# Sparse attention and a feed-forward layer on one core: where and when the later weights are converted, and in which order the first loads go out

## The chip, the cores and the metric

The kernel runs on one core of a Trainium2 chip. A core has five engines with a queue of instructions each: TensorE (PE in the profile, with its weight loads as PEld), VectorE (DVE), ScalarE (ACT), GpSimd (POOL) and SyncE (SP, which only issues DMAs). Sixteen DMA engines move data between DRAM and the on-chip memory; SP, ACT and POOL each issue into a queue of their own. The metric is the device time of one execution in microseconds; of several executions the median counts.

## The reference, cut to what matters

```python
# q, k, v: (4 batches, 8 heads, 768 positions, 64); blocks of 32 positions, 24 to a batch
scores = scale * np.matmul(q, k.transpose(0, 1, 3, 2))
mask = np.abs(blk_i - blk_j) <= 1                       # a query block sees its neighbours,
mask = mask | (blk_i == 0) | (blk_j == 0) | (blk_i == 23) | (blk_j == 23)   # the two end blocks,
for qb in range(24):                                    # and three sampled blocks
    for kb in sampled_blocks[qb]:
        mask[qb*32:(qb+1)*32, kb*32:(kb+1)*32] = True
attn = softmax(np.where(mask, scores, -1e9))
x = (attn @ v) as 3072 tokens x 512
h = x @ w_in                                            # 512 x 2048
g = np.maximum(h, 0.0) + np.log1p(np.exp(-np.abs(h)))
return g @ w_out                                        # 2048 x 512
```

`w_in` and `w_out` are double precision; everything else is single. The first and the last query block of each batch see all keys.

## The kernel before, in words

**Attention.** A batch has six *places*: groups of four query blocks (the last has two), and the first and last query block are handled together as a seventh *set* of the batch, marked `whole`. That makes 28 sets. Each set is worked in two *units* of four heads, 56 in all, and each unit in three *pieces*: `score_piece` (`scores`: matmuls on the neighbours straight from the keys `kT` and on a gathered tile `kg`, then the masking reduction on DVE), `value_piece` (`exponents` on ACT, then `values`, matmuls with `vg`) and `transpose_piece` (`normalise`, `transposes`, whose copies from PSUM go half to ACT and half to DVE). Pieces of neighbouring units overlap: score of unit n + 2 beside values of unit n.

POOL gathers. For each query block it copies three sampled key blocks from `kT` into `kg` (L461); the end blocks' keys are copied for the first two places of each batch (L451). For V it issues an indirect DMA per query block (L498) into the `vg` tile of the set, with row numbers from `ix` (`make_index`). Beside that SP loads the neighbours' rows of V (L489) and, into partitions 96 to 127, block 0 (L492); the fourth group of 32 rows of each gather is the last block of V. `vg` has two buffers in the pool `wk`.

**Feed-forward.** Tokens are worked in eight tiles of 384 (three places each). A hidden *unit* is one tile times one of sixteen slices f of the 2048 hidden columns: 12 matmuls `h` (L208 to L210), the softplus on ACT and DVE, and 9 matmuls `o` (L265 to L267) three units later (`LEAD`). Each single-precision operand is split into a high and a low part, and three products are taken. The *first pass* runs slices 0 to 5 (`EARLY`) of all eight tiles: 48 units, between which the attention pieces that make the next tile of x are placed (`due`); partial outputs go to DRAM (`yD`), and so do the x tiles (`xD`). The *second pass* runs slices 6 to 15 on x tiles read back: 80 units. In program order the loop over j emits `first_half(j)`, attention pieces that are due, `second_half(j)`, more pieces.

**Weights.** A *half* is one slice of one matrix, 128 x 512 double-precision words, 512 KB. `Weights` turns it into two single-precision parts: a raw load (L125), two ACT operations (`words`, L132 and L135), three DVE operations (`assemble`, L140, L144, L147), an integer add on POOL (L151), a cast on ACT (`high`, L157) and a subtraction (`low`, L163: DVE for the early slices, POOL for the later ones). `step` alternates between load, high and words for successive halves, and low and assemble. The 12 early halves are converted from the start on, one step per call of `convert` (one after each attention piece, two per j), their loads issued on ACT's queue. When they are done, their buffers are given up and the second batch's keys are loaded in their place (`kT[1]`). The 20 later halves are converted after the attention, when its memory is free, at 3.4 steps per unit (`HALVES`), straight into tiles of the pool `w2`.

**The start.** 22 attention pieces go before the first hidden unit (`needs[0]`). The order of the first loads is written out by hand ahead of the loop.

Of the kernel before, what the change touches and what calls it, by code (L numbers as in the profile page):

```python
# [19 lines left out]
BLOCK = 32  # L20
# [15 lines left out]
HALVES = 3.4  # L36
# [3 lines left out]
def sparse_attention_ffn(  # L40
# [20 lines left out]

    nc = tc.nc
    B, NG, P, NP, NI, _ = q.shape
    NB = k.shape[1]
# [29 lines left out]
    convctx = ctx.enter_context(ExitStack())  # L94
# [6 lines left out]
    yD = [dram.tile([P, DM], F32, name=f"yD{n}") for n in range(len(order))]  # L101

# [4 lines left out]
    class Weights:  # L107
# [5 lines left out]
        def __init__(self, halves, engine, ahead, late):  # L113

            self.halves, self.engine, self.ahead, self.late = halves, engine, ahead, late
            self.at = 0
            self.raw, self.t, self.r = {}, {}, {}
# [4 lines left out]
        def load(self, h):  # L122
            f, which = self.halves[h]
            raw = pools["conv"].tile([P, DM], I64, tag="raw", name=f"raw{which}{f}", bufs=self.ahead + 1)
            self.engine.dma_start(out=raw, in_=w_out[f * P : (f + 1) * P, :] if which else w_in[f])  # L125
            self.raw[h] = raw

        def words(self, h):
            f, which = self.halves[h]
            self.t[h] = pools["conv"].tile([P, DM], F32, tag="wt", name=f"wt{which}{f}", bufs=self.late + 1)  # L130

            nc.scalar.activation(self.t[h], self.view(h, F32)[:, :, 1], AF.Abs)  # L132
# [4 lines left out]
        def assemble(self, h):  # L137
            ti = self.t[h].bitcast(I32)
# [4 lines left out]

            nc.vector.tensor_scalar(  # L144
                out=ti, in0=ti, scalar1=3, scalar2=0x3FFFFFFF, op0=ALU.logical_shift_left, op1=ALU.bitwise_and
            )
            nc.vector.scalar_tensor_tensor(  # L147
# [3 lines left out]
            nc.gpsimd.tensor_tensor(out=ti, in0=ti, in1=self.r[h], op=ALU.add)  # L151

        def high(self, h):
            f, which = self.halves[h]
            pool = w1 if f < EARLY else pools["w2"]
            W[which, f] = [pool.tile([P, DM], F32R, name=f"w{x}{which}{f}") for x in range(2)]
            nc.scalar.copy(out=W[which, f][0], in_=self.t[h])  # L157

        def low(self, h):
            f, which = self.halves[h]  # L160
            hi, lo = W[which, f]
            eng = nc.gpsimd if f >= EARLY else nc.vector
            eng.tensor_tensor(out=lo, in0=self.t[h], in1=hi.bitcast(F32), op=ALU.subtract)  # L163
# [12 lines left out]

        def done(self):
            return self.at >= 2 * (len(self.halves) + self.ahead + self.late)
# [121 lines left out]
    pools["conv"] = convctx.enter_context(tc.tile_pool(name="conv", bufs=2))  # L300
# [9 lines left out]
    ixf = ac.tile([P, NB], F32, name="ixf")  # L310
    ix = ac.tile([P, B, NB], I32, name="ix")
# [15 lines left out]
    nc.vector.memset(ixf[NR * BLOCK : P], float((LAST - NR) * BLOCK))  # L327
    nc.vector.tensor_copy(out=iuf, in_=iu)
    nc.vector.tensor_copy(out=iof, in_=io)
# [19 lines left out]
    def make_index():  # L349

        for s in range(NR + 1):
            rows = slice(s * BLOCK, (s + 1) * BLOCK)
            if s == NR:
                nc.vector.tensor_scalar(
# [532 lines left out]
```

## Time and profile before

| | |
|---|---|
| time, median of 3 runs | 914.66 us (912.77 to 917.05) |
| the profiled execution | 920.34 us, span 918.6 us |
| PE busy | 814.6 us (89%) |
| PE weight loads | 676.6 us (74%) |
| DVE busy | 601.7 us (66%) |
| ACT busy | 466.8 us (51%) |
| POOL busy | 248.7 us (27%) |
| DMA | 127.44 MB, mean 139 GB/s |
| mean granted TensorE clock | 0.949 |

Busy times are of one execution, and the shares are of its span. A share over the whole span averages stages with different limits: the start with attention alone, the first pass with attention and hidden units mixed, a stretch in which the later weights are converted, and the rest of the second pass. Where a view lists waits, it gives the waiting instruction, what ended the wait, the total, the count and the longest.

### The profile page before, as it was taken

To read this page: it belongs to the slowest core of one execution; us is meant where nothing else is said; L and a number is where in the kernel's file an instruction comes from. 1 tells how busy PE (TensorE), PEld (TensorE's weight loads), DVE (VectorE), ACT (ScalarE), POOL (GpSimd) and SP (SyncE) were. 2 spreads that over 40 slices of the span, in tenths; PEclk is the share of its full clock that TensorE was granted. 3 is DMA by queue.
4 is the path that set the end of the run, shared out by engine and by line. 5 is a ranking of instruction groups with operands and counts; after the bars stand their busy time and mean duration, and the time that the engine had idled before them with its cause. 6 is when DMAs were issued, how large, how long until landed. Compare 5 with 4: busy or idle time off the path is not lost.

```text
span 918.6 us, 23764 instructions
## 1 busy us (share of the span) xinstructions
PE 814.6 (89%) x9438; PEld 676.6 (74%) x9438; DVE 601.7 (66%) x1460; ACT 466.8 (51%) x1133; POOL 248.7 (27%) x432
## 2 busy tenths in 40 slices
PE   3656889999988999999999877689999999999998
PEld 2434567777767777787678665678989898999986
DVE  1577756566556566565665999986666665656564
ACT  0556655564555555555464655544444444444442
POOL 2787163432443422544000455630000000000000
PEclk6777999999999999999999977799999999999999
DMA  9588747773387842867324526212121230312021
GB/s 197 179 246 244 243 129 213 197 220 135 116 217 196 232 164 70 221 195 207 142 82 161 195 99 243 70 70 70 68 69 70 70 118 23 135 66 73 1 69 35
DMA packets 58239, 127.44 MB, mean 139 GB/s; under 512 B 5264, under 2 KB 17680, under 8 KB 58128
## 3 DMA queue, kind: packets, MB, share of 16 engines
q1 hardware_dynamic: 47648, 95.70, 33.9%
q0 software_dynamic: 7040, 23.07, 8.3%
q10 hardware_dynamic: 3440, 7.15, 2.6%
q8 instruction: 74, 1.21, 0.6%
q14 instruction: 37, 0.30, 0.1%
HBM read 100.74 MB, written 25.17 MB: 137 GB/s over the span
## 4 chain that ended last, share of the span: by engine, by line
PE 70%; DVE 16%; ACT 4%; issue 2%; POOL 1%; DMA 0%; POOLq 0%; ACTq 0%; DVEq 0%
PE h L208 9%; PE h L209 9%; PE h L210 9%; PE o L265 9%; PE o L267 8%; PE o L266 8%; PE s L538 6%; PE x L635 4%; PE t L604 3%; DVE wt L147 2%; DVE gl L243 2%; DVE wt L144 2%; DVE u L219 2%; PE s L559 2%; DVE pr L541 1%
## 5 line engine op out<-in xcount | busy, mean ns | idle before, releaser
L267 PE MATMUL o<-w,gl 128*128 128x512 f32 x384 | 158.4, 412 | 27.3 <-DVE gl L243 27.3
L208 PE MATMUL h<-x,w 128*128 128x384 f32 x512 | 179.9, 351 | 1.5 <-DVE e L222 1.5
L209 PE MATMUL h<-x,w 128*128 128x384 f32 x512 | 174.9, 342 | 2.2 <-issue 2.2
L210 PE MATMUL h<-x,w 128*128 128x384 f32 x512 | 174.3, 340 | 0.0
L265 PE MATMUL o<-w,gh 128*128 128x512 f32 x384 | 158.4, 412 | 2.0 <-DVE os L284 2.0
L591 ACT ACTIVATE pr<-pr,nmax 128x256 f32<-128x256 f32 (+2 forms) x208 | 110.0, 531 | 89.4 <-DVE nmax L541 65.3
L266 PE MATMUL o<-w,gh 128*128 128x512 f32 x384 | 154.7, 403 | 0.0
L212 ACT ACTIVATE e<-h 128x384 f32<-128x384 f32 x128 | 62.7, 490 | 175.3 <-PE h L210 173.5
L541 DVE CUSTOM_DVE_ANT_1 pr<-s,mask 128x256 f32<-128x256 f32 (+1 forms) x192 | 70.0, 419 | 105.2 <-PE s L538 87.2
L219 DVE TENSOR_SCALAR u<-e 128x384 f32<-128x384 f32 x128 | 59.1, 461 | 95.0 <-ACT e L213 95.0
L498 POOL DMA_INDIRECT vg<-in_v_dram,ix x88 | 87.7, 996 | 112.6 <-PE x L635 88.4
L267 PEld LDWEIGHTS o<-w,gl 128*128 128x128 f32 x384 | 74.6, 194 | 49.3 <-DVE gl L243 31.7
L208 PEld LDWEIGHTS h<-x,w 128*128 128x128 f32 x512 | 99.2, 194 | 11.4 <-issue 3.3
L209 PEld LDWEIGHTS h<-x,w 128*128 128x128 f32 x512 | 98.9, 193 | 4.1
L210 PEld LDWEIGHTS h<-x,w 128*128 128x128 f32 x512 | 98.2, 192 | 2.3 <-issue 2.3
L237 ACT CAST gh<-l 128x384 fp32r<-128x384 f32 x128 | 65.7, 513 | 65.1 <-PE o L266 63.2
L461 POOL COPY kg<-kT 128x128 f32 x264 | 77.7, 333 | 67.0 <-PE s L538 65.3
L265 PEld LDWEIGHTS o<-w,gh 128*128 128x128 f32 x384 | 73.7, 192 | 20.5 <-issue 6.0
L243 DVE TENSOR_TENSOR gl<-l,gh 128x384 fp32r<-128x384 f32 x128 | 83.8, 655 | 0.6 <-ACT gh L237 0.6
L266 PEld LDWEIGHTS o<-w,gh 128*128 128x128 f32 x384 | 73.9, 193 | 13.0
L538 PE MATMUL s<-kg,qc 64*32 64x160 f32 x1408 | 66.0, 325 | 18.8 <-POOL kg L461 15.1
L233 DVE TENSOR_TENSOR l<-l,e 128x384 f32<-128x384 f32 x128 | 71.0, 555 | 14.7 <-ACT l L228 14.4
(78 smaller groups left out, 1173.4 us busy)
## 6 DMA issues: line engine op xcount, KB each, us to landing
vg<-in_v_dram SPq DMA_DIRECT2D x20, 768.0 KB
xD<-x SPq DMA_DIRECT2D x16, 768.0 KB
x<-xD SPq DMA_DIRECT2D x16, 768.0 KB
qc<-in_q_dram SPq DMA_DIRECT2D x24, 256.0 KB
vg<-in_v_dram SPq DMA_DIRECT2D x12, 512.0 KB
yD<-os SPq DMA_DIRECT2D x24, 256.0 KB
y<-yD SPq DMA_DIRECT2D x24, 256.0 KB
kT<-in_k_dram SPq DMA_DIRECT2D x14, 384.0 KB
```

The lines of the kernel that those rows point to most:

```text
L208: nc.tensor.matmul(ph, wh[:, cols], hi[:, c], start=(c == 0), stop=False)
L209: nc.tensor.matmul(ph, wh[:, cols], lo[:, c], start=False, stop=False)
L210: nc.tensor.matmul(ph, wl[:, cols], hi[:, c], start=False, stop=(c == NC - 1))
L243: nc.vector.tensor_tensor(out=gl, in0=l, in1=G[n].bitcast(F32), op=ALU.subtract)
L265: nc.tensor.matmul(po[m], gh[:, cols], wh, start=first, stop=False)
L266: nc.tensor.matmul(po[m], gh[:, cols], wl, start=False, stop=False)
L267: nc.tensor.matmul(po[m], gl[:, cols], wh, start=False, stop=last)
L461: eng.tensor_copy(out=kd[:, i, 1 + s, :], in_=kT[b][:, bass.ds(x, 1), :].rearrange("p n f -> p (n f)"))
L498: nc.gpsimd.indirect_dma_start(out=vd[:, 1, i, :], out_offset=None, in_=v, in_offset=bass.IndirectOffsetOnAxis(ap=ix[:, b, 4 * g + 1 + i : ...
L538: nc.tensor.matmul(o, qd[half, p, i, :], src, start=True, stop=True)
L541: nc.vector.tensor_tensor_reduce(out=pr[r][rows, j], in0=ps[r][rows, j], in1=mask[rows, g].unsqueeze(2).to_broadcast([ni * BLOCK, NS, BLOCK]),
L591: nc.scalar.activation(x, x, AF.Exp, bias=nmax[rows, r, j : j + 1], scale=-1.0, accum_out=rs[rows, h : h + 1])
```

## The change

- All 32 halves are one list, converted from the start through the first pass in *ticks*, four to a half, each stage of a half at a tick of its own: magnitude (0), last places and clamp (1), shift (2), assemble (3), load of the half after next (5), high (6), store of the high part (7), low (8), store of the low part (9). While the early halves last there is one tick per call of `convert` (`EARLY_TICKS`), after them half a tick (`LATE_TICKS`). The operation on the low words writes in place; `low` is on DVE for all halves; all raw loads are issued on SP.
- The two parts of each later half are stored to DRAM (`wD`, `park`). When the attention has ended, they are loaded into `w2`, two slices per unit (`load_w2`), from six units before the second pass on. The first x tile is read back three units ahead instead of two.
- The keys lie in DRAM by partition, so that a part of six blocks is 3 KB in a row. The second batch's keys are loaded during units 5 and 6.
- The index of the V gathers is built ahead of the mask, and the first loads of V, raw weights and queries go out in another order. ACT copies the end keys for the first two places.
- `vg` becomes two fixed buffers; the end blocks of V are loaded into partitions 96 to 127 for the first two places of a batch only, and the gathers write 96 rows.
- The DMA scratch of POOL's descriptors is set to 2048 bytes.

```diff
...
-HALVES = 3.4
+EARLY_TICKS = 1.0
+LATE_TICKS = 0.5
...
+    wD = {
+        (which, f): [dram.tile([P, DM], F32, name=f"wD{x}{which}{f}") for x in range(2)]
+        for f in range(EARLY, NF) for which in range(2)
+    }
...
-            raw = pools["conv"].tile([P, DM], I64, tag="raw", name=f"raw{which}{f}", bufs=self.ahead + 1)
-            self.engine.dma_start(out=raw, in_=w_out[f * P : (f + 1) * P, :] if which else w_in[f])
+            first = h < self.extra
+            raw = pools["extra" if first else "conv"].tile(
+                [P, DM], I64, tag="raw", name=f"raw{which}{f}", bufs=self.extra if first else 2
+            )
+            nc.sync.dma_start(out=raw, in_=w_out[f * P : (f + 1) * P, :] if which else w_in[f])
...
-        def words(self, h):
...
-            self.t[h] = pools["conv"].tile([P, DM], F32, tag="wt", name=f"wt{which}{f}", bufs=self.late + 1)
...
-            self.r[h] = pools["conv"].tile([P, DM], I32, tag="wr", name=f"wr{which}{f}", bufs=self.late)
-            nc.scalar.activation(self.r[h], self.view(h, U32)[:, :, 0], AF.Copy, scale=2.0**-29)
...
+        def last_places(self, h):
+            nc.scalar.activation(
+                self.view(h, I32)[:, :, 0], self.view(h, U32)[:, :, 0], AF.Copy, scale=2.0**-29
+            )
+        def clamp(self, h):
...
+        def shift(self, h):
+            ti = self.t[h].bitcast(I32)
...
+        def assemble(self, h):
+            ti = self.t[h].bitcast(I32)
             nc.vector.scalar_tensor_tensor(
                 out=ti, in0=self.view(h, I32)[:, :, 1], scalar=TOP2, in1=ti, op0=ALU.bitwise_and, op1=ALU.bitwise_or
             )
-            nc.gpsimd.tensor_tensor(out=ti, in0=ti, in1=self.r[h], op=ALU.add)
+            nc.gpsimd.tensor_tensor(out=ti, in0=ti, in1=self.view(h, I32)[:, :, 0], op=ALU.add)
...
             f, which = self.halves[h]
-            pool = w1 if f < EARLY else pools["w2"]
-            W[which, f] = [pool.tile([P, DM], F32R, name=f"w{x}{which}{f}") for x in range(2)]
+            if f < EARLY:
+                W[which, f] = [w1.tile([P, DM], F32R, name=f"w{x}{which}{f}") for x in range(2)]
+            else:
+                hi = pools["conv"].tile([P, DM], F32R, tag="wh", name=f"wh{which}{f}", bufs=1)
+                W[which, f] = [hi, self.t[h].bitcast(F32R)]
             nc.scalar.copy(out=W[which, f][0], in_=self.t[h])
         def low(self, h):
+            hi, lo = W[self.halves[h][::-1]]
+            nc.vector.tensor_tensor(out=lo, in0=self.t[h], in1=hi.bitcast(F32), op=ALU.subtract)
+        def park(self, x, h):
             f, which = self.halves[h]
-            hi, lo = W[which, f]
-            eng = nc.gpsimd if f >= EARLY else nc.vector
-            eng.tensor_tensor(out=lo, in0=self.t[h], in1=hi.bitcast(F32), op=ALU.subtract)
-        def step(self):
-            n = len(self.halves)
-            at, second = divmod(self.at, 2)
-            for stage, lag in (
-                ((self.low, self.ahead + self.late), (self.assemble, self.ahead)) if second
-                else ((self.load, 0), (self.high, self.ahead + self.late), (self.words, self.ahead))
+            if f >= EARLY:
+                nc.sync.dma_start(out=wD[which, f][x], in_=W[which, f][x].bitcast(F32))
+        def tick(self):
+            for stage, at in (
+                (lambda h: self.park(0, h), 7), (lambda h: self.park(1, h), 9),
+                (lambda h: self.load(h + 2), 5),
+                (self.low, 8), (self.high, 6),
+                (self.assemble, 3), (self.shift, 2), (self.clamp, 1),
+                (self.last_places, 1), (self.magnitude, 0),
             ):
-                if 0 <= at - lag < n:
-                    stage(at - lag)
+                h, rest = divmod(self.at - at, 4)
+                if rest == 0 and 0 <= h < len(self.halves) - (2 if at == 5 else 0):
+                    stage(h)
             self.at += 1
         def done(self):
-            return self.at >= 2 * (len(self.halves) + self.ahead + self.late)
+            return self.at > 4 * (len(self.halves) - 1) + 9
...
-    ixf = ac.tile([P, NB], F32, name="ixf")
-    ix = ac.tile([P, B, NB], I32, name="ix")
+    ixf = ac.tile([NR * BLOCK, NB], F32, name="ixf")
+    ix = ac.tile([NR * BLOCK, B, NB], I32, name="ix")
...
+    nc.vector.tensor_copy(out=iof, in_=io)
...
     def make_index():
...
+    vbuf = [ac.tile([P, 2, NI, DM], F32, name=f"vg{n}") for n in range(2)]
...
+    def end_keys(m, copy):
+        for slot, blkno in ((0, 0), (NR + 1, LAST)):
+            copy(
+                out=kg[m % 2][:, :, slot, :],
+                in_=kT[order[m][0]][:, blkno : blkno + 1, :].to_broadcast([P, NI, NP * BLOCK]),
+            )
...
-            if i == 0 and m % NG < 2:
-                for slot, blkno in ((0, 0), (NR + 1, LAST)):
-                    eng.tensor_copy(
-                        out=kd[:, :, slot, :],
-                        in_=kT[b][:, blkno : blkno + 1, :].to_broadcast([P, NI, NP * BLOCK]),
-                    )
+            if i == 0 and 2 <= m and m % NG < 2:
+                end_keys(m, eng.tensor_copy)
...
-        vd = vg[sets[m]] = wk.tile([P, 2, NI, DM], F32, tag="vg", name=f"vg{m}")
+        vd = vg[sets[m]] = vbuf[m % 2]
...
-        nc.sync.dma_start(
-            out=vd[3 * BLOCK : P, 0, 0:ni],
-            in_=v[b * S : b * S + BLOCK].unsqueeze(1).to_broadcast([BLOCK, ni, DM]),
-        )
+        if g < 2:
+            for c, lo in enumerate((b * S, (b + 1) * S - BLOCK)):
+                nc.sync.dma_start(
+                    out=vd[3 * BLOCK : P, c],
+                    in_=v[lo : lo + BLOCK].unsqueeze(1).to_broadcast([BLOCK, NI, DM]),
+                )
...
-                out=vd[:, 1, i, :],
+                out=vd[0 : 3 * BLOCK, 1, i, :],
...
-            if i < 4 and 0 < b < B - 1:
+            if b == 0 and i in (5, 6):
+                load_kT(1, 2 * i - 10)
+                load_kT(1, 2 * i - 9)
+            elif i < 4 and 0 < b < B - 1:
                 load_kT(b + 1, i)
...
+    early = sorted(((f, which) for f in range(EARLY) for which in range(2)), key=lambda x: (x[0] + LEAD * x[1], x[1]))
+    later = [(f, which) for f in range(EARLY, NF) for which in range(2)]
+    extractx = ExitStack()
+    pools["conv"] = ctx.enter_context(tc.tile_pool(name="conv", bufs=1))
+    pools["extra"] = extractx.enter_context(tc.tile_pool(name="extra", bufs=1))
+    weights = Weights(early + later, 3)
...
     unpack_blocks()
+    make_index()
+    make_mask()
     load_keys(0)
-    make_mask()
     load_values(0)
     load_queries(1)
+    weights.load(0)
+    end_keys(0, nc.scalar.copy)
     scores(0)
-    make_index()
     gathered(value_work, 0)
+    load_values(1)
+    weights.load(1)
+    load_queries(2)
     load_keys(1)
     scores(1)
     exponents(0)
-    load_values(1)
-    load_queries(2)
+    end_keys(1, nc.scalar.copy)
     load_keys(2)
     load_queries(3)
-    early = [(0, 0), (1, 0)] + [x for f in range(2, EARLY) for x in ((f - 2, 1), (f, 0))]
-    early += [(f, 1) for f in (EARLY - 2, EARLY - 1)]
-    weights = Weights(early, nc.scalar, 1, 1)
-    weights.step()
-    weights.step()
+    for h in range(2, 5):
+        weights.load(h)
...
+    owed = 0.0
     def convert():
-        if weights.done():
-            return
-        weights.step()
-        if weights.done() and w2 is None:
-            convctx.close()
-            pools["kv2"] = kv2.enter_context(tc.tile_pool(name="kv2", bufs=1))
-            for n in range(4):
-                load_kT(1, n)
-            load_keys()
+        nonlocal owed
+        owed += EARLY_TICKS if weights.at < 4 * len(early) + 9 else LATE_TICKS
+        while owed >= 1 and not weights.done():
+            weights.tick()
+            owed -= 1
+            if weights.at == 4 * weights.extra + 2:
+                extractx.close()
+                pools["kv2"] = kv2.enter_context(tc.tile_pool(name="kv2", bufs=1))
...
-    def convert_to(j, x):
-        if w2 is None:
-            convert()
-        else:
-            while not weights.done() and weights.at < HALVES * (j - late_from + x):
-                weights.step()
+    def load_w2(f):
+        for which in range(2):
+            W[which, f] = [pools["w2"].tile([P, DM], F32R, name=f"w{x}{which}{f}") for x in range(2)]
+            for x in range(2):
+                nc.sync.dma_start(out=W[which, f][x].bitcast(F32), in_=wD[which, f][x])
+    ahead = None
...
-        if j == SECOND - 2:
+        if j == SECOND - 3:
             load_x(0)
         first_half(j)
         while done < len(attention) and done < due(j + 0.5):
             attend()
-        convert_to(j, 0.5)
+        convert()
...
-        convert_to(j, 1)
-        if done == len(attention) and w2 is None:
+        convert()
+        if done == len(attention) and ahead is None:
+            assert weights.done(), weights.at
             actx.close()
             kv2.close()
             pools["w2"] = ctx.enter_context(tc.tile_pool(name="w2", bufs=1, side="right"))
...
-            late_from = j + 1
+            ahead = EARLY
+        while ahead is not None and ahead < min(NF, EARLY + 2 * (j + EARLY - SECOND + 1)):
+            load_w2(ahead)
+            ahead += 1
...
-        "k": k.reshape(B, NP, 2, NB, BLOCK, D).transpose(0, 3, 2, 5, 1, 4).reshape(B, NB, 2 * D, NP * BLOCK),
+        "k": k.reshape(B, NP, 2, NB, BLOCK, D).transpose(0, 2, 5, 3, 1, 4).reshape(B, 2 * D, NB, NP * BLOCK),
...
-    nc = _bacc.Bacc("TRN2", target_bir_lowering=False, num_devices=1)
+    nc = _bacc.Bacc("TRN2", target_bir_lowering=False, num_devices=1, dynamic_dma_scratch_size=2048)
...
```

More of the change, by code (lines that the diff above doesn't have):

```diff
@@ L63, in sparse_attention_ffn @@
     B, NG, P, NP, NI, _ = q.shape
-    NB = k.shape[1]
+    NB = k.shape[2]
     S = NB * BLOCK
@@ L93, in sparse_attention_ffn @@
     pools = {}
-    convctx = ctx.enter_context(ExitStack())
     ident = const.tile([P, P], F32, name="ident")
@@ L107, in sparse_attention_ffn, with __init__ @@
     class Weights:
-        def __init__(self, halves, engine, ahead, late):
-            self.halves, self.engine, self.ahead, self.late = halves, engine, ahead, late
+        def __init__(self, halves, extra):
+            self.halves, self.extra = halves, extra
             self.at = 0
-            self.raw, self.t, self.r = {}, {}, {}
+            self.raw, self.t = {}, {}
+            self.loaded = 0
         def view(self, h, dt):
@@ L122, in load, with magnitude @@
         def load(self, h):
+            if h < self.loaded:
+                return
+            self.loaded = h + 1
             f, which = self.halves[h]
-            raw = pools["conv"].tile([P, DM], I64, tag="raw", name=f"raw{which}{f}", bufs=self.ahead + 1)
-            self.engine.dma_start(out=raw, in_=w_out[f * P : (f + 1) * P, :] if which else w_in[f])
+            first = h < self.extra
[3 more added lines that the diff above has]
+            nc.sync.dma_start(out=raw, in_=w_out[f * P : (f + 1) * P, :] if which else w_in[f])
             self.raw[h] = raw
-        def words(self, h):
+        def magnitude(self, h):
             f, which = self.halves[h]
-            self.t[h] = pools["conv"].tile([P, DM], F32, tag="wt", name=f"wt{which}{f}", bufs=self.late + 1)
+            self.t[h] = pools["conv"].tile([P, DM], F32, tag="wt", name=f"wt{which}{f}", bufs=3)
             nc.scalar.activation(self.t[h], self.view(h, F32)[:, :, 1], AF.Abs)
-            self.r[h] = pools["conv"].tile([P, DM], I32, tag="wr", name=f"wr{which}{f}", bufs=self.late)
-            nc.scalar.activation(self.r[h], self.view(h, U32)[:, :, 0], AF.Copy, scale=2.0**-29)
-        def assemble(self, h):
-            ti = self.t[h].bitcast(I32)
+        def last_places(self, h):
[3 more added lines that the diff above has]
+        def clamp(self, h):
             nc.vector.tensor_scalar(
@@ L299, in sparse_attention_ffn @@
     wk = actx.enter_context(tc.tile_pool(name="wk", bufs=2, side="right"))
-    pools["conv"] = convctx.enter_context(tc.tile_pool(name="conv", bufs=2))
     blk = ac.tile([P, NB * NR * 2], I32, name="blk")
@@ L349, in make_index @@
     def make_index():
-        for s in range(NR + 1):
+        for s in range(NR):
             rows = slice(s * BLOCK, (s + 1) * BLOCK)
-            if s == NR:
-                nc.vector.tensor_scalar(
-                    out=ixf[rows], in0=ixf[rows], scalar1=iof[rows, 0:1], scalar2=None, op0=ALU.add
-                )
-                continue
             nc.vector.tensor_scalar(
@@ L398, in load_kT @@
         part = slice(n * 6, n * 6 + 6)
-        engine.dma_start(out=kT[b][:, part], in_=k[b, part].rearrange("n p f -> p n f"))
+        engine.dma_start(out=kT[b][:, part], in_=k[b, :, part])
     def overlapping(src, lo, n, rows):
@@ L844, in sparse_attention_ffn @@
             pools["w2"] = ctx.enter_context(tc.tile_pool(name="w2", bufs=1, side="right"))
-            pools["conv"] = ctx.enter_context(tc.tile_pool(name="conv2", bufs=2))
-            w2 = weights = Weights([(f, which) for f in range(EARLY, NF) for which in range(2)], nc.sync, 3, 2)
             late[0] = True
-            late_from = j + 1
+            ahead = EARLY
+        while ahead is not None and ahead < min(NF, EARLY + 2 * (j + EARLY - SECOND + 1)):
+            load_w2(ahead)
+            ahead += 1
 _BLOCKS = 24
```

7 lines of the change are left out of this document (1 added, 6 removed).

## The prediction

> **What bounds the kernel now.** I read the summary and its slices first, then each engine's busy time by stage, then the waits and the chain of work wherever TensorE (PE) is not full.
>
> ```profile
> span 918.6 us, 23764 instructions
> ...
> PE   3656889999988999999999877689999999999998
> ...
> PEclk6777999999999999999999977799999999999999
> ```
>
> Each digit is a fortieth of the span. PE is full except in two places: the first five slices, and three slices beyond the middle. The stages, cut where the first hidden unit starts (94 us), where the conversion of the later weights starts to bite (508.9) and where it ends (607.5); columns are window, length, busy time of each engine, granted clock, DMA share, GB/s:
>
> ```profile
> 37.00:94.00 57.00, 36.69 (x967) 27.00 (x964) 41.95 (x114) 35.86 (x95) 43.62 (x67) 0.80 0.79 234
> 94.00:135.00 41.00, 34.11 (x559) 25.64 (x550) 27.42 (x83) 22.43 (x60) 14.57 (x31) 0.92 0.58 181
> 135.00:496.00 361.00, 338.47 (x5884) 267.93 (x5874) 221.21 (x684) 195.19 (x547) 118.34 (x250) 1.00 0.59 171
> 508.90:607.50 98.60, 69.32 (x258) 58.15 (x257) 96.50 (x119) 57.17 (x110) 55.98 (x39) 0.82 0.40 142
> 607.50:906.00 298.50, 298.50 (x1489) 269.42 (x1488) 191.83 (x380) 139.88 (x287) 1.39 (x1) 1.00 0.20 69
> ```
>
> The same windows for the first activation of each hidden unit alone (one per unit, both ends counted):
>
> ```profile
> 508.90:607.50 98.60, 5.66 (x13) 0.82 0.40 142
> 607.50:906.00 298.50, 35.16 (x72) 1.00 0.20 69
> ```
>
> A unit costs 298.5/71 = 4.20 us when PE sets the pace. In the conversion stage twelve units took 98.6 us, 8.2 each, with VectorE (DVE) busy 96.5 of 98.6 us. The chain of work there (start, length, what) is DVE throughout, after one wait for a DMA:
>
> ```profile
> 509.15 3.33 DMA raw<-in_w_in_dram
> ...
> 515.07 1.41 DVE wt L144
> 516.50 1.67 DVE wt L147
> ...
> 518.65 1.54 DVE gl L243
> 520.19 1.36 DVE u L219
> ```
>
> One conversion, operation by operation (min/median/max in ns):
>
> ```profile
> L132 ACT ACTIVATE wt<-raw x32: 642/675/716, 29.8 to 597.3; 128x512 f32<-128x512 f32 x32
> L140 DVE TENSOR_SCALAR wt<-wt x32: 415/420/510, 39.1 to 600.1; 128x512 f32<-128x512 f32 x32
> L144 DVE TENSOR_SCALAR wt<-wt x32: 426/427/1400, 39.6 to 600.6; 128x512 int32<-128x512 int32 x32
> L147 DVE SCALAR_TENSOR_TENSOR wt<-raw,wt x32: 691/693/1673, 40.1 to 602.0; 128x512 int32<-128x512 int32 x32
> L151 POOL TENSOR_TENSOR wt<-wt,wr x32: 1249/1308/1447, 40.9 to 603.8; 128x512 int32<-128x512 int32 x32
> L157 ACT CAST w<-wt x32: 600/618/642, 42.2 to 608.4; 128x512 fp32r<-128x512 f32 x32
> L163 DVE TENSOR_TENSOR w<-wt,w x12: 684/742/877, 43.4 to 105.6; 128x512 fp32r<-128x512 f32 x12
> ```
>
> **The change part by part.** Five terms; the sum is made against the profiled execution (920.3 us, span 918.6), which is 5.7 us above the median of the three timed runs (914.7). Those runs lie 0.5% apart, so a difference under 0.5% can't be told from none.
>
> (a) *Until the first value product.* GpSimd (POOL) and PE, start, length, and the idle time before with its releaser:
>
> ```profile
> 16.67 0.61 POOL L451 COPY kg<-kT 128x512 f32<-128x512 f32 x1 [7.66 <-DMA kT<-in_k_dram]
> 17.78 1.54 POOL L461 COPY kg<-kT 128x128 f32 x6 [0.49 <-issue]
> ...
> 26.84 1.15 POOL L498 DMA_INDIRECT vg<-in_v_dram,ix  x1 [5.13 <-DVE ix L364]
> ...
> 31.75 1.16 POOL L451 COPY kg<-kT 128x512 f32<-128x512 f32 x2
> 32.86 2.88 POOL L461 COPY kg<-kT 128x128 f32 x12
> ...
> 37.32 1.70 PE L635 MATMUL x<-vg,pt 128*32 128x64 f32 x50
> ```
>
> Keys land at 16.7 us in rows of 512 bytes. The new layout makes them rows of 3 KB; query, block table and keys are some 1.9 MB, 8 us at the 234 GB/s above and about 2 us of start, so I put the landing at 10 to 11 us: 6 earlier. Building the index ahead of the mask removes the 5.13 us wait (about 2 us of small DVE work moves ahead of the mask, which the keys' landing covers). Copying the end keys on ScalarE (ACT) takes 0.61 + 1.16 us off POOL; ACT is idle then. Together 13. Less, because more DMA is now asked for sooner (end blocks of V for the first two sets are 512 KB instead of 256, and three raw halves are spread in): bounds 4 and 13; I take 10, nearer the POOL rows, which are a chain.
>
> (b) *From there to the first hidden unit,* 57 us for 22 attention pieces, POOL the busiest (43.6). Waits (total, times, longest) and POOL's groups:
>
> ```profile
> PEld s L538 <- ACT pt L612: 19.5, 7, 5.3
> ACT w L157 <- POOL wt L151: 18.4, 9, 3.8
> ...
> L498 POOL DMA_INDIRECT vg<-in_v_dram,ix x16 | 17.3, 1080 | 2.7 <-issue 2.4
> L151 POOL TENSOR_TENSOR wt<-wt,wr 128x512 int32<-128x512 int32 x12 | 15.2, 1265 | 17.3 <-DVE sums L663 11.6 <-DVE wt L147 5.7
> ```
>
> PE waits for ACT, and ACT's cast waits for POOL's add, which stands behind gathers. Before, a half takes two steps, one per piece; now four ticks. Those 22 pieces carry about six halves fewer: POOL 6 x 1.27 = 7.6 us, ACT 6 x 1.97 = 12 (and the issues of the raw loads, which go to SP), DVE 6 x 2.28 = 14. The cast also comes three ticks after the add instead of one, so the 18.4 us mostly goes. The gathers write 96 rows instead of 128; I count nothing for that. What is late next is DMA (0.79 busy): a place before asks for 256 KB of queries, 2 MB of V and three halves of 512 KB; after, 256 KB, 1.5 to 2 MB and one and a half halves, so it asks for less. Bounds 0 (DMA sets it already) and 18; I take 11, about POOL's saving and a part of the wait. The six halves are done beside the first seven units instead, at a tick per call.
>
> (c) *The first four units,* 94 to 135: PE is busy 83%, against 94% in the next stage; 11% of 41 us is 4.4. Part of it is the second batch's keys, loaded only after all early conversions; now they are loaded during units 5 and 6 of the first batch. Bounds 0 and 8; I take 4.
>
> (d) *The first pass, which takes on 20 halves.* Each has 0.42 + 0.43 + 0.69 + 0.74 = 2.28 us of DVE (the subtraction moves there from POOL, where it took 1.5), 1.97 of ACT, 1.31 of POOL, a raw load and two park stores. DVE goes from 221 to 267 us of 361 (61 to 74%), ACT from 54 to 65%. POOL keeps slack. What PE itself waits for in this pass (150 to 475 us), and POOL's own waits:
>
> ```profile
> POOL vg L498 <- PE x L635: 85.6, 13, 27.4
> ...
> PE s L538 <- issue: 4.7, 13, 1.5
> ...
> PE x L635 <- issue: 3.8, 4, 2.9
> PE s L538 <- ACT pt L612: 3.5, 5, 1.0
> ```
>
> PE's idle time is 361 - 338.5 = 22.5 us, about half of it issue. If the other half grows as busy/(1-busy) of DVE, 1.56 to 2.85, it becomes 20: 9 more, and 3 for ACT: 12. That is an estimate; the bounds are 0 (the work fits the gaps; no gain, since PE hardly waits for POOL or DMA) and the price per half in the second pass, 48 us for 20 halves (below). I take 12, since with 26% of DVE free the stage is nearer the one it is than the one with none. V's fixed end blocks remove 11.4 MB and add 4.2; raw loads and parks add 21: some 48 GB/s over 290 us, to 219, under the 234 that ran at 0.79. On SP a park waits for the cast or subtraction just ahead in program order, and the V, query and raw loads behind it are a set or more ahead of need. ACT's next cast reuses the one buffer of high parts, so it waits for that store's landing; three ticks at half a tick per call are six calls, the 152 pieces left and two calls for each of 42 units are 236 calls in 400 us, so 10 us of cover. I count nothing; without the cover it is rival 4. The smaller descriptor scratch I cost at nothing too: POOL's gathers waited 2.4 us on issue in all of (b), and its slack covers some more; were each gather held 1 us, the sixteen in (b) would use up that term, which its bound of 0 includes.
>
> The trace bears on one contention: L144 ran 427 ns in the first stage and 1400 in the second pass, where POOL's add and POOL's subtraction ran back to back. The Trainium skill, SBUF — State Buffer, section Who interferes with whom, says that a DVE instruction with two SBUF inputs or in a two-port mode and a GpSimd one exclude each other for a whole instruction. By that rule each of the 20 adds may hold DVE 1.31 us, DVE is 81% busy, (d) 23 and the time 867; the first stage's rows show next to none of it.
>
> (e) *The second pass.* 98.6 - 12 x 4.20 = 48 us go, the conversions having left. In their place weights are read back, and the first x tile stands behind six of ten of their pairs in SP's order:
>
> ```profile
> 492.45 1.97 SPq L702 DMA_DIRECT2D xD<-x  x2
> 494.65 0.33 SPq L125 DMA_DIRECT2D raw<-in_w_in_dram  x1
> ```
>
> By window again:
>
> ```profile
> 494.00:500.00 6.00, 6.00 (x32) 5.59 (x32) 3.55 (x8) 2.46 (x6) 0.00 (x0) 1.00 1.00 358
> ...
> 510.00:520.00 10.00, 7.66 (x39) 6.66 (x37) 9.79 (x13) 7.59 (x15) 5.17 (x5) 1.00 0.60 200
> ```
>
> Ahead of the end of that tile's landing go 1.6 MB of x stored, 6.3 of weights, 0.8 of y and its own 1.6: 10.2 MB, 29 us at 358 GB/s from 492.5, so 521; the second pass begins seven units after 494, at 523. Some wait after the y stores: 2 us. At 200 GB/s it is 51 us and a wait of 20. I take 2, since nothing else then loads DMA: 46 gained.
>
> The sum: -10 - 11 - 4 + 12 - 46 = -59: 861 for the profiled execution, 856 by the median.
>
> **The rivals.**
> 1. *The price only moves:* each half costs in the first pass the 2.4 us it cost in the second. For it: in-order DVE and ACT put each operation ahead of some piece's. Against: 140 us of free DVE there, two of 98.6 in the second pass. Term (d) 48: 892.
> 2. *The start does not shorten,* because DMA, 0.79 busy, sets it: (a) and (b) 0: 877. Against: the waits above name POOL and ACT, not DMA.
> 3. *Read-back is late:* 200 GB/s instead of 358, (e) 28: 874.
> 4. *Slower than before:* ACT held at its cast of each of 19 halves until the park store of the half before lands. It eats all 59 us at 3.1 us each, that is when a store takes 13 us instead of under 10; at 4 us each it is 914.7 - 59 + 76 = 932. Against: 219 GB/s is below what the queue carried.
> 5. *Better:* (a) 13, (b) 18, (c) 8, (d) 0, (e) 48: 828. That the change doesn't do what it says is small: 57 calls for the early halves and 154 for the later ones are 211 of the 258 there are (236 and the first 22), so conversion ends in time.
>
> **How the numbers follow.** My forecast 0.50; rival 1 0.15; 2 0.15; 3 0.08; 4 0.05; 5 0.07. The time is that of the forecast, 856. The range 830 to 890 leaves out rival 4 and about half of rivals 1 and 5, 0.16 together. Faster 0.94, the same 0.02, slower 0.04, all but rival 4 being well below 910.
>
> **What would show it.** First hidden unit at 66 to 80 us instead of 94 and no index wait on POOL (a, b); no wait of POOL for keys between units 0 and 3 (c); PE busy over 90% between there and the end of attention, DVE near 75% (d); units of 4.2 us from there to the end with one gap under 5 us where the second pass begins (e). Wrong if: waits of ACT's cast for a DMA, DVE over 85% in the first pass, units above 4.3 us after attention, or a clock below 1.00 inside the first pass.

## The result: faster by 3.7%, with 23 us of the forecast missing

The changed kernel took 879.5 us in the median of four runs (875.3 to 883.8), the kernel before 913.7 beside it: a ratio of 0.963, 95% interval 0.956 to 0.969. The forecast was 856, its range 830 to 890. The profiled execution took 881.3 us (before: 920.3), so the profiles differ by 39 us where the medians differ by 34; the profile of before ran 6 us above its median.

The page of the changed kernel, the lines that answer to those shown of before:

```profile
span 879.5 us, 23879 instructions
...
PE   5677776999888999979999998999999999999997
...
PEclk6899878999999999998999999999999999999999
```

The dip beyond the middle is gone but for one digit (slice 25); the start is shorter; a new dip stands in slices 5 to 7 (88 to 154 us), where the clock is lower than it was, and a single 7 in slice 18. The stages, cut where the first value product starts (30.7 us; 37.3 before), at the first activations of hidden units 0, 6 and 41, and around the one wait of the second pass (columns as in the prediction):

```profile
30.70:74.10 43.40, 32.73 (x1046) 25.81 (x1045) 33.98 (x103) 28.14 (x81) 34.74 (x62) 0.95 0.75 213
74.10:162.60 88.50, 66.17 (x974) 50.65 (x980) 62.28 (x162) 49.94 (x131) 39.64 (x68) 0.81 0.63 196
162.60:501.10 338.50, 312.61 (x5374) 247.92 (x5365) 252.41 (x697) 207.88 (x551) 135.83 (x237) 0.98 0.66 204
501.10:526.40 25.30, 25.30 (x128) 22.80 (x128) 15.62 (x31) 12.77 (x27) 0.00 (x0) 1.00 0.87 311
526.40:533.80 7.40, 4.63 (x22) 3.69 (x21) 2.50 (x5) 1.91 (x4) 0.00 (x0) 1.00 1.03 397
533.80:866.20 332.40, 332.40 (x1661) 300.05 (x1660) 209.84 (x417) 155.84 (x319) 0.00 (x0) 1.00 0.22 79
```

The same two cuts of the first pass before the change (units 0 to 6, units 6 to 41):

```profile
96.60:163.80 67.20, 58.45 (x1040) 45.21 (x1046) 43.02 (x133) 37.31 (x107) 28.31 (x61) 0.95 0.65 191
163.80:496.20 332.40, 311.73 (x5374) 246.41 (x5366) 203.33 (x625) 179.59 (x499) 104.61 (x220) 1.00 0.57 167
```

Laid side by side, the 39 us come out as follows. The forecast's terms have slightly other bounds: (b) ended at the first matmul of a hidden unit, (c) covered four units, and (d) all of the first pass behind them.

| stage | before | after | difference | forecast |
|---|---|---|---|---|
| to the first value product | 37.3 | 30.7 | -6.6 | (a) -10 |
| to the first activation of unit 0 | 59.3 | 43.4 | -15.9 | (b) -11 |
| units 0 to 6 | 67.2 | 88.5 | +21.3 | (c) -4 |
| units 6 to 41 | 332.4 | 338.5 | +6.1 | (d) +12 |
| unit 41 to the end | 422.4 | 378.4 | -44.0 | (e) -46 |

Unit 6 is reached at 162.6 us instead of 163.8: nearly all that the start gained is given back beside the first six units. There PE is idle for 22.3 us instead of 8.8, and it is busy 7.7 us longer, at a clock of 0.81 instead of 0.95, although one value product (64 matmuls `x`) fell ahead of the cut. The 24 matmuls of one line of `h` show it, before and after:

```profile
L209 PE MATMUL h<-x,w 128*128 128x384 f32 x24 | 8.2, 342 | 0.0
...
L237 PE MATMUL h<-x,w 128*128 128x384 f32 x24 | 10.3, 428 | 0.0
```

The waits from 72 to 172 us (total, times, longest):

```profile
POOL wt L172 <- DVE wt L168: 19.8, 7, 7.1
...
ACT wt L145 <- DMA raw<-in_w_out_dram: 11.3, 3, 4.5
...
PEld s L567 <- ACT pt L641: 8.4, 4, 7.6
DVE wt L155 <- ACT wt L145: 7.8, 3, 5.0
PE s L567 <- ACT pt L641: 7.6, 2, 7.4
```

And the chain of work there (start, length, what):

```profile
70.82 11.71 DMA raw<-in_w_out_dram
82.56 0.72 ACT wt L145
83.30 0.43 DVE wt L155
83.73 0.28 DVE u L247
...
122.20 0.40 DVE wt L162
122.62 0.69 DVE wt L168
123.32 0.60 DVE w L185
123.92 1.57 DVE l L261
125.49 0.47 DVE gl L271
...
136.72 11.35 DMA raw<-in_w_out_dram
148.10 0.66 ACT wt L145
...
151.33 0.50 ACT pt L641
151.82 0.04 issue
151.87 2.10 PE s L567 x64
```

Both views offer the same suspect, raw loads that land 11 to 12 us after their issue and on which ACT stands. Behind the second one stands PE's longest gap of the stage, the wait of 7.4 us for ACT in the list. But the middle piece of the chain has another suspect: three conversion operations on DVE in front of the softplus of a hidden unit (`l`, `gl`, `u`, `e`), on which the next matmuls wait.

### The profile page after: what moved, and what is told of

It is laid out like the page before. It is cut to its first block, busy times and chain, and to the rows that moved or that the text cites. A ratio compares the mean times of both kernels' runs of the same rounds, so it can differ in the third digit from the quotient of the medians.

```text
span 879.5 us, 23879 instructions
## 1 busy us (share of the span) xinstructions
PE 798.6 (91%) x9438; PEld 667.7 (76%) x9438; DVE 591.2 (67%) x1478; ACT 467.6 (53%) x1137; POOL 222.8 (25%) x408
## 4 chain that ended last, share of the span: by engine, by line
PE 69%; DVE 15%; DMA 7%; ACT 4%; issue 3%; POOL 1%; POOLq 0%; SPq 0%; ACTq 0%; DVEq 0%
PE h L236 10%; PE h L237 10%; PE h L238 10%; PE o L293 9%; PE o L295 9%; PE o L294 8%; PE s L567 6%; PE t L633 3%; DMA raw<-in_w_out_dram 3%; DVE pr L570 2%; PE x L664 2%; DVE e L249 2%; DVE gl L271 2%; DVE l L261 1%; PE s L588 1%
## 5 line engine op out<-in xcount | busy, mean ns | idle before, releaser
L293 PE MATMUL o<-w,gh 128*128 128x512 f32 x384 | 156.7, 408 | 0.0
L295 PE MATMUL o<-w,gl 128*128 128x512 f32 x384 | 153.6, 400 | 0.0
L294 PE MATMUL o<-w,gh 128*128 128x512 f32 x384 | 152.9, 398 | 0.0
L247 DVE TENSOR_SCALAR u<-e 128x384 f32<-128x384 f32 x128 | 49.2, 384 | 117.0 <-ACT e L241 117.0
L527 POOL DMA_INDIRECT vg<-in_v_dram,ix x88 | 86.3, 981 | 83.9 <-PE x L664 63.7
L487 POOL COPY kg<-kT 128x128 f32 x264 | 81.7, 348 | 62.3 <-PE s L567 52.2
L261 DVE TENSOR_TENSOR l<-l,e 128x384 f32<-128x384 f32 x128 | 75.7, 592 | 18.0 <-ACT l L256 18.0
L293 PEld LDWEIGHTS o<-w,gh 128*128 128x128 f32 x384 | 72.8, 189 | 19.1 <-issue 6.4
L294 PEld LDWEIGHTS o<-w,gh 128*128 128x128 f32 x384 | 73.0, 190 | 12.6
L567 PE MATMUL s<-kT,qc 64*32 64x96 f32 x1408 | 48.5, 271 | 33.3 <-ACT pt L641 18.9
L271 DVE TENSOR_TENSOR gl<-l,gh 128x384 fp32r<-128x384 f32 x128 | 77.0, 602 | 0.6 <-ACT gh L265 0.6
```

The source lines that it names most:

```text
L261: nc.vector.tensor_tensor(out=l, in0=l, in1=e, op=ALU.add)
L271: nc.vector.tensor_tensor(out=gl, in0=l, in1=G[n].bitcast(F32), op=ALU.subtract)
L293: nc.tensor.matmul(po[m], gh[:, cols], wh, start=first, stop=False)
L294: nc.tensor.matmul(po[m], gh[:, cols], wl, start=False, stop=False)
L295: nc.tensor.matmul(po[m], gl[:, cols], wh, start=False, stop=last)
L527: nc.gpsimd.indirect_dma_start(out=vd[0 : 3 * BLOCK, 1, i, :], out_offset=None, in_=v, in_offset=bass.IndirectOffsetOnAxis(ap=ix[:, b, 4 * ...
```

## The experiments

Two theories. *Supply*: raw loads come late and hold ACT. *Work*: the conversion's own operations, put in front of attention and softplus on in-order queues, cost PE time wherever they stand. Each run is timed against the kernel before on its own chip; a ratio has 0.3 to 0.7% to either side, about 5 us, and a difference of two ratios somewhat more. A stage is read from one profile of each run, and it scatters: in four runs that convert exactly what the change converts (loads one tick earlier, loads by POOL, V as before, keys as before), units 0 to 6 took 82.7, 88.1, 82.6 and 83.9 us, against 88.5 with the change, and none of the four was faster. Differences of 6 us in this stage alone show nothing. The changed kernel stands at 0.963, and since the chips differ a little, differences from it are given by the ratios, times 914 us.

**No raw loads.** In `load`:

```diff
...
+            if h >= 5:
+                self.raw[h] = self.raw[3 + (h - 3) % 2]
+                return
...
```

> Leaves out the loads of raw halves 5 to 31: they are converted from the two buffers loaded last, so the weights are not the reference's. Everything else stays, every conversion operation too. Theory supply (the conversions beside units 0 to 6 are held by raw loads that come late: the buffer is freed by POOL's add, then the load stands in SP's queue behind x stores, V and keys; ACT stands at the first operation on a raw half, and everything behind it on ACT): units 0 to 6 take 66 to 72 us instead of 88.5, the time falls by 15 to 24 us, to 856 to 865. Theory work (the conversion operations themselves are too much for DVE and ACT there): units 0 to 6 stay at 84 us or more, the time falls by under 5 us.

875.1 us, 0.960 (0.953 to 0.967); units 0 to 6 in 82.2 us, between the two expectations. 3 us below the change is inside both intervals. Supply falls as the main cause: with no load to wait for, most of the loss is still there, though a wait of 11 us was printed for it. It is not nothing: PE's longest wait for ACT in this stage is 2.8 us here instead of 7.4, and unit 6 is reached 5.4 us earlier.

**No DVE operations.**

```diff
...
-                (self.assemble, 3), (self.shift, 2), (self.clamp, 1),
+                (self.add_low, 3),      # POOL's add alone
...
```

> Leaves out clamp, shift and assemble, the three DVE operations of 1.55 us in all, for every half; the weights are not the reference's. Raw loads, ACT's operations, POOL's add and the stores stay. Theory supply: loads come as late as before but for POOL's add, which no longer waits for DVE; the time falls by 3 to 10 us, units 0 to 6 stay above 78 us. Theory work: units 0 to 6 fall to 72 us or less and the time by 15 us or more.

871.8 us, 0.957 (0.952 to 0.961), some 5 us less than the change; units 0 to 6 in 79.5 us, units 6 to 41 in 331.1, 9 and 7 us less than with the change in the profiles. Both numbers lie where theory supply put them (3 to 10 us, above 78), not where theory work did (15 us or more, 72 or less). So the three DVE operations are a part, seen in both stages, and not the whole; this run does not tell the theories apart, the next two do.

**Loads one tick earlier, and loads by POOL.**

```diff
...
-                (lambda h: self.load(h + 2), 5),
+                (lambda h: self.load(h + 2), 4),
...
```

```diff
...
-            nc.sync.dma_start(out=raw, ...
+            eng = nc.sync if h < 5 else nc.gpsimd
+            eng.dma_start(out=raw, ...
...
```

> Each raw load is asked for one tick earlier (tick 4 instead of 5 of the half two before, the tick after POOL's add). Theory supply: four ticks instead of three to cover the landing, 2 to 3 us more for each, so 4 to 10 us less in all, if SP is not held by the add itself; 0 if it is. Theory work: no change within 2 us.

> Raw loads from half 5 on are issued by POOL one tick after its add (tick 4) instead of by SP at tick 5: nothing in SP's queue stands ahead of them, and SP does not wait for the add. POOL pays about 1 us for each of 27. Theory supply: the time falls by 8 to 18 us. If the DMA engines as such are full there (theory bandwidth), the loads land as late and the time falls by under 4 us. Theory work: no fall, or 1 to 5 us slower for POOL's work.

882.0 us, 0.967 (0.962 to 0.973), and 884.3 us, 0.969 (0.963 to 0.975; this one has the earlier tick too). Neither is told apart from the change. Supply would have had both faster.

**Six early halves left out.** From here the question was whether the conversion as a whole is the cause, or something else in the change.

```diff
...
+                if 6 <= h < 2 * EARLY and rest == 0:
+                    if at == 6:
...
+                        W[which, f] = W[which, 0]
+                    if at != 5:
+                        continue
...
```

> Leaves out everything of halves 6 to 11 (loads, ACT, DVE, POOL): slices 1 to 5 use the parts of the first half of the same matrix where these are missing, so the output is not the reference's. The halves after 11 stay. After the runs without raw loads (units 0 to 6 in 82 us instead of 88) and without the DVE operations (80), each theory again. Theory work, now as the sum of all a half's operations on three in-order queues: units 0 to 6 take 65 to 71 us as before the change, the time falls by 16 to 22 us. Theory elsewhere (the end blocks of V, the earlier keys, the order of loads, not the conversion): units 0 to 6 stay above 79 us and the time falls by under 6 us.

868.8 us, 0.954 (0.951 to 0.957): some 8 us less than the change, half of the 16 that theory work asked for at least and more than the other theory allowed. By window, units 0 to 6 and 6 to 41:

```profile
76.70:149.30 72.60, 58.74 (x969) 44.09 (x975) 46.23 (x137) 39.89 (x113) 30.65 (x61) 0.91 0.65 190
149.30:485.20 335.90, 310.11 (x5374) 246.12 (x5372) 252.76 (x698) 208.01 (x551) 135.40 (x238) 0.99 0.67 205
```

Units 0 to 6 lose 15.9 us, DVE's busy time there 16 and ACT's 10; PE's own busy time is back at 58.7. The stage is near what theory work gave (65 to 71), and far from the 79 of the other: the loss in this stage is the conversion, loads and operations together. That the time fell by half as much as the stage is in part the scatter of the stage (88.5 is the longest of its kind).

**The later halves left out**, their stores kept.

```diff
...
+                if h >= 2 * EARLY and at not in (7, 9):
+                    continue
...
-                nc.sync.dma_start(out=wD[which, f][x], in_=W[which, f][x].bitcast(F32))
+                nc.sync.dma_start(out=wD[which, f][x], in_=W[which, f % EARLY][x].bitcast(F32))
...
```

> Leaves out the raw loads and all operations of the 20 later halves; parts of the early halves are stored in their place at the same ticks and read back, so the output is not the reference's. It shows what the conversion costs in the first pass behind unit 6 (units 6 to 41 took 338.6 us, 6.2 more than before the change). Theory work with slack there: 4 to 10 us less. If rival 1 of the prediction holds in part (the stage would be faster than before without it): 15 us less or more.

854.0 us, 0.938 (0.934 to 0.943): 22 us less than the change, which is near the forecast of 856. By window:

```profile
77.60:151.70 74.10, 59.20 (x963) 45.39 (x971) 56.93 (x153) 45.69 (x124) 37.68 (x65) 0.88 0.66 202
151.70:474.60 322.90, 307.12 (x5374) 246.71 (x5372) 203.65 (x625) 179.84 (x499) 104.33 (x220) 0.99 0.61 187
```

Twenty later halves cost about 22 us, 1.1 each; in the profiles it is 15.6 behind unit 6 and 14.4 ahead of it, where the first of them meet the last early ones, and where the raw load behind PE's gap of 7.4 us is theirs. That is more than the 6 us by which that stage lies above before. Without conversion the stage behind unit 6 ran 9.5 us below before, which no term had; part of it may be scatter, as the profile of before is 6 us above its median.

This run and the one before it together give 30 us for 26 halves. What was taken away one part at a time, the raw loads (3), three DVE operations (5 to 6) and, below, two ACT operations (6 to 7), gives 15 for all halves. The cast, the subtraction and POOL's add were never left out alone; half of the price has no part named for it by a run.

**Faster and slower ticks.** Two ticks per call while the early halves last; then three in four calls from the 22nd tick on; then the same with 0.42 instead of 0.5 for the later halves and the loads at tick 4.

```diff
...
-EARLY_TICKS = 1.0
+EARLY_TICKS = 2.0
...
```

> Two ticks per call instead of one while the early halves last: the rate of the kernel before, two steps to a half. Theory work: the work goes back into the start, which lengthens by 8 to 14 us, and units 0 to 6 fall to 66 to 74 us; the time moves by under 6 us either way. Theory elsewhere: the start lengthens by 8 to 14 us, units 0 to 6 stay above 79 us, the time rises by 6 us or more.

```diff
...
+        owed += 1.0 if weights.at < 22 else EARLY_TICKS if ...   # EARLY_TICKS = 0.75
...
```

> Three ticks in four calls instead of one per call from the 22nd tick to the end of the early halves; the later ones end some 15 calls later. Theory work: the same work over nine units instead of six and a half; units 0 to 6 fall by 4 to 9 us, units 6 to 12 rise by 0 to 5, the time falls by 1 to 6 us. Theory elsewhere: no change within 2 us.

```diff
...
-LATE_TICKS = 0.5
+LATE_TICKS = 0.42       # with 0.75 as above, and the loads at tick 4
...
```

> The change with conversion spread over all the calls there are: three ticks in four calls from the 22nd tick on, 0.42 instead of 0.5 afterwards, raw loads one tick earlier. If the price of a half falls when its operations stand further apart: 3 to 9 us faster than the change. If each operation costs the same wherever it stands: within 3 us of it.

Two ticks: 888.6 us, 0.975 (0.971 to 0.980), slower than the change by about 12 us, twice what theory work allowed, with units 0 to 6 near the 66 to 74 it named. The start and units 0 to 6 by window:

```profile
31.00:98.10 67.10, 38.53 (x986) 30.26 (x988) 46.61 (x126) 36.09 (x96) 46.17 (x72) 0.76 0.73 216
98.10:173.80 75.70, 60.16 (x1033) 45.58 (x1041) 57.51 (x153) 46.85 (x124) 36.05 (x64) 0.93 0.71 218
```

The start grows by 23.7 us, units 0 to 6 shrink by 12.8: packed into attention alone, the halves cost more than beside hidden units. Three in four: 877.5 us, 0.963 (0.960 to 0.966), units 0 to 6 in 84.1 us. Spread over all calls: 0.963 (0.958 to 0.968). Both equal the change, where theory work had asked for 1 to 6 us less of the first: the price of a half did not fall when its operations stood further apart. In the second, units 0 to 6 took 76.0 us and the time did not move; the cost went behind unit 6. Beside it the same stages of the run with V as before, which ran on the same chip:

```profile
154.90:511.90 357.00, 321.44 (x5374) 252.70 (x5375) 257.58 (x706) 211.52 (x558) 142.28 (x237) 0.98 0.64 197
...
165.50:510.10 344.60, 317.54 (x5374) 249.52 (x5375) 252.02 (x697) 208.09 (x551) 135.07 (x235) 0.99 0.69 215
```

Units 0 to 6 were 6.6 us shorter, units 6 to 41 were 12.4 longer. This was the version meant to beat the change, and it does not.

**No ACT operations** (magnitude and last places); **V as before; keys as before.** These three and the spread version ran on a chip where the kernel before took 924.8 us, so only ratios are compared.

```diff
...
-                (self.last_places, 1), (self.magnitude, 0),
+                (self.magnitude, 0),       # which only takes a buffer; clamp reads the raw words
...
```

> Leaves out two of ACT's three operations on a half (magnitude and last places, 1.34 of 1.97 us) for all halves; DVE's clamp reads the raw words, POOL adds zeros, so the weights are not the reference's, and a raw buffer is free one engine earlier. Without the three DVE operations (1.55 us a half) the time fell by 8 to 10 us. Theory: the price of a half is the sum of what it puts in front of pieces on each in-order queue, ACT's like DVE's: 6 to 14 us less. Rival: DVE alone sets it (75% busy): under 4 us less.

0.955 (0.951 to 0.960), 0.7% or 6 us below the change: at the low end of what the sum over queues gives, above what DVE alone gives, with intervals that touch. (The 8 to 10 us that its expectation names for the run without the DVE operations are 5 to 6 by the ratios.)

```diff
...
-                out=vd[0 : 3 * BLOCK, 1, i, :],
+                out=vd[:, 1, i, :],        # and block 0 loaded for every set
...
```

> Undoes the fixed end blocks of V: block 0 is loaded for every set again and the gathers write 128 rows, 7.2 MB more in all. Without the later conversion units 6 to 41 took 322.9 us, 9.5 less than before the change, which no term of the prediction had. If V's traffic is where that comes from, units 6 to 41 rise by 5 to 12 us and the time by 5 to 15. If V is hidden, as the prediction had it, both stay within 3 us.

0.966 (0.960 to 0.972), 3 us above the change and inside its interval; units 6 to 41 took 344.6 us, 6 more than with the change, on a chip that is 1.2% slower, which makes 4 of them. V's fixed end blocks are not shown to bring anything, and the 9.5 us are not shown to come from them.

```diff
...
-        engine.dma_start(out=kT[b][:, part], in_=k[b, :, part])
+        engine.dma_start(out=kT[b][:, part], in_=k[b, part].rearrange("n p f -> p n f"))
...
```

> Undoes the layout of the keys alone (rows of 512 bytes). By term (a) the keys land 5 to 6 us later, the first value product comes at 34 to 37 us instead of 30.7, and the time rises by 3 to 7 us. If the start catches up (DMA sets it anyway): under 2 us.

0.970 (0.965 to 0.975), 0.75% or 7 us above the change, intervals touching. Its first key copy on POOL:

```profile
17.45 1.53 POOL L487 COPY kg<-kT 128x128 f32 x6 [15.28 <-DMA qc<-in_q_dram]
```

That is 6.2 us behind the one of the change (11.21 below), and the first value product comes at 39.0 us instead of 30.7, later than the 34 to 37 expected and than the 37.3 before the change. In the other runs on this chip it comes at 30.8 to 32.0. So with the old layout nothing of (a) is left: the index built earlier and the end keys copied by ACT show no gain without it.

## Why the prediction was right and where it was not

Direction, range and the second pass were right; the likeliest time was 23 us too low, and most of that stands in one stage, whose extra work was given no price.

**(e) held.** Units run at 4.21 us from 41 on, but for one that takes 3.3 us more where the second pass begins (forecast 2): the fifth row of the stages shows PE at 4.63 of 7.40 us with the DMA engines full at 397 GB/s. Of PE's idle time there the list for 520 to 540 us names the x tile for one half; the other, 1.3 us, it puts down to "issue":

```profile
PE h L237 <- DMA x<-xD: 1.4, 1, 1.4
```

**(a) by its mechanism, 3 us short.** POOL's first gathers after the change:

```profile
11.21 1.53 POOL L487 COPY kg<-kT 128x128 f32 x6 [9.03 <-DMA kT<-in_k_dram]
...
21.46 1.11 POOL L527 DMA_INDIRECT vg<-in_v_dram,ix  x1 [6.31 <-DVE nmax L570]
```

The keys are there at 11.2 us, near the 10 to 11 worked out. But the gather of V still waits 6.31 us; the index wait was replaced, not removed. The profile names a DVE operation that has nothing to do with V; what it waited for was not settled. **(b) was better** by 5 us: 43.4 us for the pieces. Some of that is luck, as this is the shortest of all runs; most of the others have 45 to 48.

**(c) and the last sentence of (b) failed.** "The six halves are done beside the first seven units instead, at a tick per call" was given no price and no cover was named for it. Units 0 to 6 were forecast at 67 - 4 = 63 us and took 88.5. Leaving those six out takes 15.9 us from the stage and 8 from the time, leaving the later halves out takes 14.4 from the stage; if the two add up, 58 would remain (no run left out both). The sign named for (c), no wait of POOL for keys between units 0 and 3, did not come either; the wait fell from 10.3 us to half:

```profile
POOL kg L467 <- DMA kT<-in_k_dram: 5.2, 1, 5.2
```

Seen from the rates: in those 24 pieces and six units a half stands at every fourth call, twice the rate of the later ones, while the softplus is already on the same two engines.

**(d) was mis-sized, and hidden by its neighbour.** The stage rose by 6 us, less than the 12 forecast, and DVE stands at 252.4/338.5 = 75%, as forecast. Yet taking the later halves away gave 22 us in all: the price per half, 1.1 us, is half of what the second pass paid (2.4), so rival 1 held by about half. The estimate counted PE's waits by DVE's free share. Against the run without the later halves, PE's idle time in this stage is 10.1 us longer (25.9 instead of 15.8), near the estimate; but PE is also busy 5.5 us longer with the same number of matmuls (312.6 instead of 307.1, clock 0.98 and 0.99), which no term had. "No gain, since PE hardly waits for POOL or DMA" is not borne out either: the stage without conversion lies below before, from a cause that stays open.

**The contention was larger than the prediction's rows showed.** The rule of the Trainium skill (SBUF — State Buffer, Who interferes with whom) does show in the first pass: `l`, two SBUF inputs on DVE, takes 1.57 us in the chain above instead of 0.55, and ends 0.4 us behind POOL's add:

```profile
123.55 1.52 POOL L172 TENSOR_TENSOR wt<-wt,raw 128x512 int32<-128x512 int32 x1 [1.18 <-DVE wt L168]
```

Over units 6 to 41, the same 36 operations `gl` before the change, after it, and without the later halves:

```profile
L243 DVE TENSOR_TENSOR gl<-l,gh 128x384 fp32r<-128x384 f32 x36 | 20.2, 560 | 0.0
...
L271 DVE TENSOR_TENSOR gl<-l,gh 128x384 fp32r<-128x384 f32 x36 | 25.7, 714 | 0.0
...
L273 DVE TENSOR_TENSOR gl<-l,gh 128x384 fp32r<-128x384 f32 x36 | 20.2, 561 | 0.0
```

With `l`, the first `e`, `u` and `sums` (2.3, 2.0, 1.4 and 2.1 us longer than before) that makes 13.3 us of DVE in this stage, all of it gone where the later halves are left out. The prediction had priced this rule at 1.31 us for each of 20 adds, and (d) at 23 by it; (d) came to 22, with about half of that hold. Whether the hold is what costs the time is not shown: the runs without DVE or ACT operations keep POOL's add (and `gl` at 635 and 701 ns), and no run moves the add alone. It is the rival that stands untested.

Rivals 2, 3 and 4 did not come: the start shortened, the read-back ran at 311 to 397 GB/s, and ACT's cast waited for a store once, for 2.8 us. Of the signs of being wrong, that one wait and the clock below 1.00 in the first pass (0.81, then 0.98) came; DVE over 85% and units above 4.3 us after attention, but for the one, did not.

## What to carry to other kernels

Work moved out of a saturated stage into one with slack is not free there: here a half cost 1.1 us beside the matmuls against 2.4 where DVE was full, and spreading the operations further apart did not lower that. That each operation delays what stands behind it on its in-order queue fits the runs without DVE and without ACT operations, which each gave back a part; half of the price they leave unexplained. When a step is moved, price it at the place where it lands, at the rate at which it lands there; the stage that took the unpriced move holds most of the miss. And a wait that the profile prints need not be worth its length: the raw loads, 11 us of printed waits on ACT from one matrix alone, were worth some 3 us, inside the scatter.

## What the runs showed of the hardware that was not expected

The clock was halved behind short gaps inside a busy stage. In units 0 to 6 after the change PE stood still for more than 2 us five times (2.6, 2.6, 2.1, 2.3 and 7.4 us), and behind each of these gaps the granted clock was 0.50 for 3 to 10 us. Three of the gaps, in brackets:

```profile
97.38 0.38 PE L567 MATMUL s<-kT,qc 64*32 64x96 f32 x3 [2.55 <-DVE pt L639]
...
127.80 0.41 PE L567 MATMUL s<-kT,qc 64*32 64x96 f32 x7 [2.29 <-DVE pt L639]
...
151.87 0.57 PE L567 MATMUL s<-kT,qc 64*32 64x96 f32 x16 [7.39 <-ACT pt L641]
```

And stretches behind and between them; the clock is the third number from the end:

```profile
82.90:96.40 13.50, 9.35 (x164) 6.43 (x154) 11.99 (x30) 12.11 (x26) 4.98 (x4) 1.00 0.58 202
96.50:103.20 6.70, 5.82 (x42) 5.22 (x43) 4.81 (x15) 0.30 (x1) 0.64 (x1) 0.50 0.16 63
...
127.20:133.90 6.70, 6.10 (x76) 5.13 (x78) 5.22 (x16) 0.00 (x0) 2.06 (x4) 0.50 0.21 68
134.10:147.60 13.50, 9.79 (x201) 8.25 (x195) 7.78 (x21) 7.08 (x22) 8.58 (x15) 1.00 0.91 217
147.70:157.80 10.10, 5.93 (x73) 4.11 (x73) 5.64 (x15) 6.85 (x18) 2.31 (x4) 0.50 0.76 261
```

Not every such gap does it: without raw loads PE stood for 2.8 us before 146.0 us, and the clock was 1.00 from 143.0 to 154.5. Nor does the sum of idle time tell the price. The change had 13.5 us more of it in this stage than before, and PE was busy 7.7 us longer; the run without DVE operations had 10.5 us more at a clock of 0.91, and PE was busy 1.8 us longer. The spread version stood for 16.7 us at 0.96, the run without the later halves for 14.9 at 0.88.
